# Query, key and value tensors laid out on the host, and sparse attention steps split in two, in a block-sparse attention and cosine-MLP kernel

## The chip, the cores and the metric

The kernel runs on one core of one Trainium2 chip. The metric is the time that the device needs for one execution, in microseconds (us), taken as the median of three runs. Lower is better. The host's own work ahead of the launch is not in it.

## The reference, cut to what matters

Attention over 4 batches, 8 heads, 768 tokens and 64 features a head, in float32. Tokens come in 24 blocks of 32. Each block of queries sees its own and its two neighbour blocks, the first and the last block, and three sampled blocks; the first and the last block of queries see everything. Behind it stands a two-layer MLP with the activation h*cos(h).

```python
scores = (q @ k.T) / sqrt(64)            # q, k, v: [4, 8, 768, 64]
mask = |blk_i - blk_j| <= 1 or blk_i in (0, 23) or blk_j in (0, 23) or blk_j in sampled_blocks[blk_i]
attn = softmax(where(mask, scores, -1e9)); x = attn @ v      # -> [3072, 512]
h = x @ w_in;  out = (h * cos(h)) @ w_out                    # w_in [512, 2048], w_out [2048, 512]
```

## The kernel before, in words

**Precision.** Every operand of a matmul is scaled by a power of two and split into two float16 parts, high and low; a product is the sum of high*high, high*low and low*high. So each stationary operand is loaded and streamed three times. The scale is found from the sum of squares (or a Gram matrix) of the tile.

**Tiles.** There are 24 query tiles of 128 rows, n = 0 to 23, six a batch: five sparse ones and a dense one (the first block and the last three). Two query tiles make one MLP step m = 0 to 11. A sparse tile has four units of two heads, a dense one eight units. A unit goes through scores (`qk`), adding the bias and taking the row maximum (`mx`, VectorE), exponential (`ex`, ScalarE), split into high and low (`ph`, `pl`), transpose (`PT`, by DMA; for the first sixteen units by TensorE, `PF`), and values (`pv`). The MLP of a step is 16 products up (`m`), the activation (`ev`, `ka`, `kb`, `sin`, `gm`, `gh`, `gl`) and 16 products down (`d`).

**Scores and values in two parts.** A sparse unit's scores are `shared_scores`, which read the neighbour and end blocks straight from the key tile `W` in tiles of 64 rows by 128 columns of the array, and `own_scores`, which read the sampled blocks from a gathered copy `Wg` in tiles of 64 by 32. Values have the same two parts, `shared_values` (128 by 128) and `own_values` (96 by 32), the latter reading V rows that GpSimd gathers by indirect DMA. Before, both parts are one step, `sparse_scores` or `sparse_values`, and `Plan.run` swaps the two inside a step where the part that comes first then has the tile shape of the work ahead of it.

**Layouts before.** q, k and v lie in HBM as the reference has them, [batch, head, token, feature], so that a row on a partition is put together from runs of 64 floats (256 bytes). The score matmul wants features on partitions. Keys of batch 0 are turned by TensorE (`KF0_0` to `KF0_5`, four float32 transposes each, L1832 through `turn32`); keys of batches 1 to 3 are scaled and split as they are into `kn` (`khi`, `klo`, 12 of each a batch) and turned by DMA (`kT`, L1353). Queries of tiles 0 to 3 are turned by TensorE (`UF`), those of tiles 4 to 23 by DMA (`uT`, L1449). A query's scale stands for one row.

**Order.** Engines take their instructions in program order. All loads, stores and DMA transposes are issued from SyncE's queue, gathers from GpSimd's. The order of all 3,183 steps is written out in the table `PLACES`, a name and its place, which `Plan.run` sorts by; buffers are dealt out in that order from the slots of `Sizes`. The numbers beside an `op` call are a planner's costs and due times; a step that has a place there is not moved by them.

Of the kernel before, what the change touches and what calls it, by code (L numbers as in the profile page):

```python
# [21 lines left out]
P = 128  # L22
BLK = 32
# [37 lines left out]
wl0 0 wc0_0 1 wc0_1 2 idx 3 const_ident 4 const_w 5 wc0_2 6 sx 7 regs2_0 8 kload0_1 9 KF0_2 10 const_samples 11 regs0_1 12 ql0 13 kload0_0 14  # L61
kload0_0#2 15 qsq0 16 kload0_1#2 17 const_pool 18 UF0 19 wsq0 20 KF0_1 21 const_a 22 kload0_2 23 kload0_2#2 24 ksq0_0 25 qsc0c 26 qsc0e 27 qsc0s 28
ql1 29 const_gidx 30 qhi0 31 ksq0_1 32 ksq0_2 33 qlo0 34 regs0_0 35 kred0 36 kall0s 37 regs3_1 38 kall0 39 ksc0c 40 ksc0e 41 vload0_0 42 regs4_1 43
qsq1 44 ksc0s 45 khi0_None_2 46 KF0_3 47 const_b1 48 vload0_2 49 KF0_4 50 qsc1c 51 KF0_5 52 khi0_None_3 53 qsc1e 54 KF0_0 55 vload0_1 56 khi0_None_1
57 qu0 58 klo0_None_2 59 khi0_None_4 60 klo0_None_3 61 khi0_None_5 62 klo0_None_1 63 vsq0_0 64 wl2 65 vsq0_1 66 khi0_None_0 67 klo0_None_4 68
klo0_None_5 69 klo0_None_0 70 vsq0_2 71 UF1 72 vred0 73 wl3 74 regs1_1 75 wgd0 76 wga0 77 vall0s 78 vall0 79 qnu0 80 ql2 81 vsc0c 82 qk0_0 83 vsc0e 84
vsc0s 85 vhi0_2 86 vlo0_2 87 wl4 88 const_b 89 wc3_0 90 mx0_0_0 91 vhi0_3 92 qk0_2 93 qk0_1 94 mx0_0_1 95 vst0_2 96 nb0_0 97 vhi0_4 98 vlo0_4 99
vhi0_5 100 vhi0_1 101 qsc1s 102 vlo0_5 103 qsq2 104 vhi0_0 105 vlo0_3 106 ex0_0_0 107 ex0_0_1 108 wl1 109 mx0_2_0 110 mx0_2_1 111 UF2 112 PF0_0_0 113
ql3 114 vst0_4 115 vlo0_1 116 PF0_0_1 117 nb0_2 118 const_n 119 ph0_0_0 120 vst0_5 121 vlo0_0 122 wc3_1 123 ex0_2_0 124 vst0_0 125 regs2_1 126 mx0_1_0
127 mx0_1_1 128 nb0_1 129 wc3_2 130 PG0_0_0 131 qk0_3 132 mx0_3_0 133 ph0_0_1 134 wc1_0 135 vst0_3 136 wc1_1 137 PG0_0_1 138 regs1_0 139 ex0_2_1 140  # L70
pg0_0_0 141 UF3 142 ex0_1_1 143 wc1_2 144 mx0_3_1 145 qsq3 146 qsc2c 147 qsc2e 148 ex0_1_0 149 qsc3c 150 vst0_1 151 wl6 152 const_c 153 wl7 154
PF0_2_0 155 pg0_0_1 156 PF0_1_0 157 ph0_2_0 158 PG0_2_0 159 qsc2s 160 wgd1 161 regs4_0 162 PF0_1_1 163 wsq1 164 wsq3 165 qsc3e 166 qhi1 167 nb0_3 168
wc7_0 169 wga1 170 qlo1 171 regs3_0 172 wc7_1 173 ex0_3_0 174 PF0_2_1 175 ex0_3_1 176 wred0 177 wall0s 178 wall0 179 wsc0c 180 qu1 181 ph0_1_0 182
PG0_1_0 183 ph0_1_1 184 ph0_2_1 185 PG0_1_1 186 qhi2 187 qsc3s 188 wsc0e 189 wsc0s 190 qnu1 191 ql4 192 qsq4 193 qsc4c 194 pg0_2_0 195 vg0_0 196
turn0_0 197 PG0_2_1 198 qsc4e 199 qsc4s 200 qk1_0 201 wc7_2 202 wl5 203 pg0_1_1 204 qu4 205 pg0_2_1 206 qk1_1 207 mx1_0_0 208 mx1_0_1 209 wc5_0 210
vg0_1 211 qlo2 212 qk1_3 213 nb1_0 214 whi2 215 mx1_1_0 216 mx1_1_1 217 qk1_2 218 qhi4 219 vi0_2 220 nb1_1 221 wsq7 222 whi0 223 vi0_0 224 wc5_1 225
wgd2 226 ex1_0_0 227 PF0_3_0 228 ex1_0_1 229 PF0_3_1 230 pg0_1_0 231 vi0_3 232 vg0_2 233 wsi0 234 vi0_1 235 qhi3 236 ex1_1_0 237 pv0_0 238 mx1_3_0 239
pv0_1 240 pv0_2 241 mx1_3_1 242 wc5_2 243 ph0_3_0 244 ph0_3_1 245 PG0_3_0 246 rs0 247 wl25 248 PG0_3_1 249 mx1_2_0 250 mx1_2_1 251 vg1_0 252 wlm0 253
wlm1 254 rr0 255 wga2 256 pg0_3_1 257 PF1_0_0 258 PF1_0_1 259 qu2 260 pg0_3_0 261 qlo4 262 qk2_0 263 wlp0 264 nb1_2 265 wsq5 266 qlo3 267 qnu4 268
pv0_3 269 vi1_0 270 ph1_0_0 271 ex1_1_1 272 ex1_2_1 273 wred4 274 wall4s 275 wl8 276 vi1_2 277 PF1_1_0 278 PG1_0_0 279 vi1_1 280 ph1_0_1 281 wall4 282  # L80
# [1933 lines left out]
```

## Time and profile before

| | |
|---|---|
| runs, median of 3 | 773.91 us (773.72 to 774.16) |
| profiled execution, its own time | 771.64 us |
| its span in the trace | 769.7 us |
| mean granted TensorE clock | 0.971 of full speed |
| busy: TensorE matmul, VectorE, ScalarE | 722.5, 618.8, 639.0 us |

The profiled execution lies 0.3% under the median; its span is what the trace covers. Busy shares are means over stages with different limits, and matmuls are pipelined, so a busy TensorE is not one at its peak. A row of a window gives the busy time of each engine in a stretch, the number of instructions, the granted clock, and the busy share of the 16 DMA engines.

### The profile page before, as it was taken

The page shows a single profiled execution, that of the slowest core. Times are in us where ns is not written, and L with a number is a line of the kernel's source. Part 1 is how long each engine was busy: PE and PEld are TensorE (multiplying, and loading weights), DVE is VectorE, ACT ScalarE, POOL GpSimd, SP SyncE. Part 2 cuts the span into 40 slices and gives each one's busy share as a digit, 9 for nine tenths or more (in the row PEclk, how much of TensorE's full clock was granted, in tenths as well). Part 3 has the DMA queues.
Part 4 walks back from the last instruction along what each step waited for, and adds up shares of the span by engine and source line. Part 5 has one row for each costly group of instructions (what it writes and reads, how often), then busy time and mean ns, then how long its engine had stood idle before and what let it go on. Part 6 is the DMA issues. An engine that isn't in the chain of part 4 may idle for free.

```text
span 769.7 us, 25139 instructions
## 1 busy us (share of the span) xinstructions
PE 722.5 (94%) x10330; PEld 497.3 (65%) x10330; DVE 618.8 (80%) x1578; ACT 639.0 (83%) x1260; POOL 98.2 (13%) x132
## 2 busy tenths in 40 slices
PE   5679998999999969999999999999999999999997
PEld 4456674667476537767576676667577776665673
DVE  4977999999979986989888798977878777776252
ACT  3789999999769987999799999989889887875152
POOL 4232102002300212010201202020202020000000
PEclk9659999999999999999999999999999999999999
DMA  9788995799959999999999999998899949366111
GB/s 215 257 228 233 251 264 114 165 235 220 189 115 183 184 156 203 222 262 160 192 213 177 223 206 233 208 185 153 158 163 184 179 95 166 100 129 105 28 42 42
DMA packets 289139, 135.41 MB, mean 176 GB/s; under 512 B 247680, under 2 KB 269312, under 8 KB 289024
## 3 DMA queue, kind: packets, MB, share of 16 engines
q1 hardware_dynamic: 283904, 118.07, 78.3%
q0 software_dynamic: 5120, 15.73, 8.4%
q8 instruction: 81, 1.33, 0.7%
q14 instruction: 34, 0.28, 0.1%
HBM read 68.23 MB, written 12.58 MB: 105 GB/s over the span
## 4 chain that ended last, share of the span: by engine, by line
PE 44%; ACT 24%; DVE 17%; DMA 9%; issue 5%; SPq 2%; DVEq 0%; ACTq 0%
PE ph L1885 18%; PE ph L1935 17%; ACT P L1586 6%; DMA xT<-n 3%; DVE P L1565 3%; ACT hs L1894 3%; ACT ring L1596 2%; DVE ring L1600 2%; PE ph L1663 2%; DMA PT<-ring 2%; ACT Wg L1359 2%; ACT g L1912 2%; DMA w<-in_moe_w_out_dram 2%; DVE hs L1917 1%; DMA U<-n 1%
## 5 line engine op out<-in xcount | busy, mean ns | idle before, releaser
L1885 PE MATMUL ph<-xT,w 128*128 128x256 f16 x2304 | 269.9, 275 | 10.1 <-DMA xT<-n 8.5
L1935 PE MATMUL ph<-w,g 128*128 128x512 f16 x1152 | 265.6, 380 | 0.2 <-DVE g L1926 0.2
L1885 PEld LDWEIGHTS <-w 128*128 128x128 f16 x2304 | 224.0, 99 | 50.7 <-issue 12.8
L1935 PEld LDWEIGHTS <-g 128*128 128x128 f16 x1152 | 108.8, 98 | 120.9 <-issue 4.8
L1586 ACT ACTIVATE P<-P,sm 128x352 f32<-128x352 f32 (+1 forms) x224 | 154.9, 698 | 4.8 <-DVE sm L1580 3.9
L1474 POOL DMA_INDIRECT V<-scr,gidx x80 | 86.4, 1080 | 523.9 <-PE ph L1647 369.5
L1600 DVE TENSOR_TENSOR ring<-P,ring 128x704 f16<-128x704 f32 (+1 forms) x96 | 86.6, 907 | 17.3 <-ACT ring L1596 16.0
L1894 ACT ACTIVATE hs<-ph,sm 128x512 f32<-128x512 f32 x96 | 62.8, 681 | 30.7 <-PE ph L1885 27.0
L1565 DVE CUSTOM_DVE_ANT_1 P<-ph,bias 128x352 f32<-128x352 f32 x160 | 79.3, 516 | 4.3 <-PE ph L1534 2.0
L1596 ACT CAST ring<-P 128x704 f16<-128x704 f32 (+1 forms) x96 | 75.1, 791 | 1.8 <-DMA PT<-ring 1.2
L1917 DVE SCALAR_TENSOR_TENSOR hs<-hs,sm,g 128x1024 f32<-128x1024 f32 x48 | 61.4, 1279 | 18.4 <-ACT g L1912 17.8
L1926 DVE TENSOR_TENSOR g<-hs,g 128x1024 f16<-128x1024 f32 x48 | 58.2, 1219 | 18.4 <-ACT g L1923 18.4
L1912 ACT ACTIVATE g<-g,sm 128x1024 f32<-128x1024 f32 x48 | 54.8, 1146 | 20.0 <-DVE g L1908 19.6
L1923 ACT ACTIVATE g<-hs 128x1024 f16<-128x1024 f32 x48 | 49.9, 1048 | 13.4 <-DVE hs L1917 13.4
L1908 DVE SCALAR_TENSOR_TENSOR g<-g,hs 128x1024 f32<-128x1024 f32 x48 | 58.4, 1220 | 0.6
L1904 DVE TENSOR_SCALAR g<-hs 128x1024 f32<-128x1024 f32 x48 | 33.1, 689 | 29.5 <-ACT hs L1894 26.8
L1586 ACT ACTIVATION_READ_ACCUMULATOR P<-P,sm 128x1 f32 x224 | 46.4, 207 | 0.0
L1526 PE MATMUL ph<-W,U 64*128 64x192 f16 (+1 forms) x960 | 42.5, 222 | 1.9 <-DVE sm L1565 1.9
L1663 PE MATMUL ph<-V,PT 128*128 128x64 f16 x960 | 42.4, 195 | 1.2 <-DMA PT<-ring 1.1
L1663 PEld LDWEIGHTS <-PT 128*128 128x128 f16 x960 | 36.4, 99 | 9.9 <-DMA PT<-ring 1.6
L1526 PEld LDWEIGHTS <-U 64*128 64x128 f16 x960 | 28.7, 96 | 17.1 <-issue 14.3
L1565 DVE CUSTOM_DVE_ANT_1 P<-ph,dbias 128x384 f32<-128x384 f32 x64 | 34.1, 551 | 4.3 <-PE ph L1549 3.8
(170 smaller groups left out, 870.2 us busy)
## 6 DMA issues: line engine op xcount, KB each, us to landing
V<-scr SPq DMA_DIRECT2D x20, 384.0 KB, 5.3
w<-in_moe_w_in_dram SPq DMA_DIRECT2D x12, 512.0 KB, 4.8
w<-in_moe_w_out_dram SPq DMA_DIRECT2D x12, 512.0 KB, 5.0
V<-scr SPq DMA_DIRECT2D x8, 768.0 KB, 4.8
scr<-n SPq DMA_DIRECT2D x21, 256.0 KB, 4.4
qs<-in_q_dram SPq DMA_DIRECT2D x20, 256.0 KB, 5.1
stage<-in_v_dram SPq DMA_DIRECT2D x9, 512.0 KB, 5.6
stage<-in_k_dram SPq DMA_DIRECT2D x9, 512.0 KB, 6.2
```

The source lines that it names most:

```text
L1474: self.nc.gpsimd.indirect_dma_start(V[:96, 2 + j, :], None, self.scr[b][:, :], bass.IndirectOffsetOnAxis(ap=self.gidx[:96, c : c + 1], axi ...
L1526: mm(out, u[r], x, start=(begins and first and not part), stop=(not begins and final and part == 1), tile_position=(a * D, 0))
L1565: self.nc.vector.tensor_tensor_reduce(out=self.p_view(n, Pt)[:, a].rearrange("p (n c) -> p n c", c=hf), in0=self.flat32(sp)[:, :w].rearran ...
L1586: self.nc.scalar.activation(Pv[:, a], Pv[:, a], AF.Exp, scale=qc[:, 4:5], bias=nb[:, a : a + 1], accum_out=sums[:, x : x + 1],)
L1596: self.nc.scalar.copy(R[:, :, 0, : self.width(n)], self.p_view(n, Pt))
L1600: self.nc.vector.tensor_tensor(R[:, :, 1, :w], self.p_view(n, Pt), R[:, :, 0, :w], ALU.subtract)
L1663: mm(xp[:, h, :], PT[:, 6 * a + 3 * l + c, :], V[:, c, h, d0:d1], start=(first and a == 0 and c == 0 and x == 0), stop=(not first and a == ...
L1885: self.nc.tensor.matmul(ph[:, ff, :], self.W1[p][:, wl, cc, c * P : (c + 1) * P], xT[:, xl * NCC + cc, :], start=(j == 0), stop=(j == len( ...
L1894: self.nc.scalar.activation(hs[:, h * 512 : h * 512 + 512], ph.rearrange("p f t -> p (f t)"), AF.Copy, scale=self.turns[b][:, p : p + 1])
L1912: self.nc.scalar.activation(kt, kt, AF.Sin, scale=-SIN_SCALE, bias=self.halfpi)
L1917: self.nc.vector.scalar_tensor_tensor(hs, hs, c[:, p : p + 1], kt, op0=ALU.mult, op1=ALU.mult)
L1935: self.nc.tensor.matmul(self.flat32(po), g[:, gl, ff, t * P : (t + 1) * P], self.W2[p][:, wl, ff, :], start=(first and ff == half * hf and ...
```

## The change

The host lays the three tensors out before the launch: q as [batch, tile, 128 partitions, 512], where a partition holds one of two heads' 64 features; k as [batch, 3, 128, 1024] with features on partitions; v as [batch, 3, 128, 1024] with tokens on partitions. A load is then one run of 2 or 4 KB a partition. All turning of q and k goes: 6 `KF`, 4 `UF`, 20 `uT`, 36 `kT`. A query tile is split straight into `U`, and keys into `W`, in 6 steps a batch for `khi` and `klo` each (12 before, for batches 1 to 3). Since a partition no longer is a query row, a query tile has one scale: its sums of squares are added over the partitions by a matmul with ones (`qsp`, 24 new steps on TensorE), whose result `row_scale` reads from PSUM. `qk` and `pv` of sparse units are two steps each (`qk`, `qo` and `pv`, `po`), placed apart; the first and the last of a PSUM bank get the start and stop flags. Slots: `qs` 1 to 2, `kn` 2 to 0, `ot` 2 and `acc` 2 to `ot` 5. `PLACES` is a new table of 3,258 steps.

```diff
-wl0 0 wc0_0 1 wc0_1 2 idx 3 const_ident 4 const_w 5 wc0_2 6 sx 7 regs2_0 8 kload0_1 9 KF0_2 10 const_samples 11 regs0_1 12 ql0 13 kload0_0 14
...
+ql1 0 idx 1 ql0 2 qsq1 3 sx 4 const_pool 5 kload0_0 6 qsq0 7 qsp0 8 qsp1 9 kload0_1 10 const_samples 11 qsc0c 12 qsc1c 13 kload0_2 14 ksq0_0 15
...
-            if not b:
-                for t in range(HT):
-                    op("SP", 0, pos + 0.01 * c, lambda st=st, c=c, t=t: e.k_load_turned(st.t, c, t), w=[(st, c * HT + t)], dma=1.0, name=f"kload{b}_{c}")
-            else:
-                op("SP", 0, pos + 0.01 * c, lambda st=st, c=c: e.kv_load(b, 0, st.t, c), w=[st], dma=1.73, name=f"kload{b}_{c}")
+            op("SP", 0, pos + 0.01 * c, lambda st=st, c=c: e.kv_load(b, 0, st.t, c), w=[st], dma=1.27, name=f"kload{b}_{c}")
...
+        for c, st in enumerate(kst[b]):
+            p_ = pos + 0.2 * c
+            op("ACT", 0.613, p_, lambda st=st, c=c: e.k_hi(b, half, c, st.t), r=[st, sk[b]], w=[(W, (half, c))], name=f"khi{b}_{half}_{c}")
+            op("DVE", 0.663, p_, lambda st=st, c=c: e.k_lo(b, half, c, st.t), r=[st, sk[b], (W, (half, c))], w=[(W, (half, c))], name=f"klo{b}_{half}_{c}")
...
+        qs, U, qc, sp = Val("qs"), Val("U"), Val("qc"), Val("ph")
+        op("SP", 0, pos, lambda: e.q_load(n, qs.t), w=[qs], dma=0.635, name=f"ql{n}")
+        op("ACT", 0.613, pos, lambda: e.q_square(qc.t, qs.t), r=[qs], w=[am], name=f"qsq{n}")
+        op("PE", 0.07, pos, lambda: e.q_sum(qc.t, sp.t), r=[am, sx], w=[sp], name=f"qsp{n}")
+        row_scale(pos, lambda x: e.q_scale(x, qc.t, sp.t), sp, (qc, "e"), qe, f"qsc{n}")
...
-            op("SP", 0, pos, lambda: e.u_transpose(U.t, qn.t), r=[qn], w=[U], dma=1.15, name=f"uT{n}")
...
-                op("PE", 0.692, pos, lambda own_first=False, j=j, sp=sp: e.sparse_scores(n, j, U.t, T["Wg"].t, [x.t for x in sp], own_first),
...
+                op("PE", 0.343, pos, lambda begins, ends, j=j, sp=sp: e.shared_scores(n, j, U.t, [x.t for x in sp], begins, ends),
...
+                op("PE", 0.158, pos + 0.01, lambda begins, ends, j=j, sp=sp: e.own_scores(j, U.t, T["Wg"].t, [x.t for x in sp], begins, ends),
...
+    def q_sum(self, c, sp):
+        one = self.one.bitcast(BF16)[:, 1:2].to_broadcast([P, P])
+        self.nc.tensor.matmul(self.flat32(sp)[:, 0:1], one, c[:, 0:1].bitcast(BF16)[:, 1:2], start=True, stop=True)
...
+def lay_out(name, a):
...
+    if name == "q":
+        a = np.roll(a, -BLK, axis=2).reshape(B, H // 2, 2, S // P, P, D)
+        a = a.transpose(0, 3, 2, 5, 1, 4).reshape(B, S // P, P, H // 2 * P)
+    elif name == "k":
+        a = a.reshape(B, H // 2, 2, S // 2, 2, D).transpose(0, 1, 2, 5, 4, 3).reshape(B, H // 2, P, S // 256, 256)
+        a = a.transpose(0, 3, 2, 1, 4).reshape(B, S // 256, P, H // 2 * 256)
```

## Rows read from the trace of the kernel before

**Rows 1.** The page: busy time of each engine, share of the span, instructions.
```profile
PE 722.5 (94%) x10330; PEld 497.3 (65%) x10330; DVE 618.8 (80%) x1578; ACT 639.0 (83%) x1260; POOL 98.2 (13%) x132
```

**Rows 2.** Windows: length; PE, PEld, DVE, ACT, POOL busy; granted clock; DMA share; GB/s.
```profile
0.00:60.00 60.00, 39.38 (x545) 29.16 (x545) 43.35 (x155) 39.94 (x95) 20.31 (x60) 0.74 0.92 235
60.00:200.00 140.00, 131.35 (x1928) 90.94 (x1927) 132.43 (x323) 136.04 (x279) 17.15 (x16) 0.99 0.85 206
200.00:220.00 20.00, 16.67 (x92) 9.54 (x91) 16.61 (x37) 12.49 (x26) 5.78 (x5) 0.91 0.92 208
...
280.00:300.00 20.00, 14.70 (x318) 11.13 (x294) 12.86 (x43) 12.50 (x29) 0.00 (x0) 0.83 1.02 167
300.00:770.00 470.00, 461.71 (x6421) 318.65 (x6417) 357.98 (x845) 383.28 (x714) 47.55 (x45) 1.00 0.86 160
```

**Rows 3.** Timeline of the first 25 us: start, us, engine, line, operation, tiles.
```profile
0.72 0.41 SPq L1755 DMA_DIRECT2D w<-in_moe_w_in_dram  x1
...
2.75 7.38 SPq L1329 DMA_DIRECT2D stage<-in_k_dram  x5
5.51 0.43 DVE L1763 TENSOR_SCALAR w<-w 128x512 int32<-128x512 int32 x1 [5.51 <-DMA w<-in_moe_w_in_dram]
...
14.24 0.61 PE L1255 MATMUL ph<-stage 128*128 128x128 bf16 x4 [0.37 <-DMA stage<-in_k_dram]
...
17.19 4.79 DVE L1244 SCALAR_TENSOR_TENSOR W<-ph,sm,W 128x256 f16<-128x256 f32 x12 [0.40 <-ACT W L1241]
...
22.43 0.51 PE L1526 MATMUL ph<-W,U 64*128 64x192 f16 x12
```

**Rows 4.** DMA issues on the page: KB each, median us from issue to landing.
```profile
w<-in_moe_w_in_dram SPq DMA_DIRECT2D x12, 512.0 KB, 4.8
...
stage<-in_k_dram SPq DMA_DIRECT2D x9, 512.0 KB, 6.2
```

**Rows 5.** Groups by shape: busy us, mean ns of one, idle before and releasers.
```profile
L1241 ACT ACTIVATE kn<-stage,sm 128x256 f16<-128x256 f32 x36 | 16.7, 498 | 3.2 <-DMA out_dram<-kn 2.5 <-DMA W<-kn 0.7
...
L1244 DVE SCALAR_TENSOR_TENSOR kn<-stage,sm,kn 128x256 f16<-128x256 f32 x36 | 16.4, 479 | 1.9 <-ACT kn L1241 1.9
...
L1244 DVE SCALAR_TENSOR_TENSOR n<-stage,sm,n 128x512 f16<-128x512 f32 x18 | 13.2, 748 | 2.0 <-ACT n L1241 1.9
L1227 ACT ACTIVATE n<-qs 128x512 bf16<-128x512 f32 x20 | 12.8, 640 | 1.4 <-DMA qs<-in_q_dram 1.4
L1241 ACT ACTIVATE n<-stage,sm 128x512 f16<-128x512 f32 x18 | 12.7, 711 | 1.9 <-DMA xT<-n 1.9
...
L1832 PE MATMUL ph<-acc,stage 128*128 128x128 f32 x24 | 5.8, 424 | 8.0 <-DMA stage<-in_k_dram 8.0
...
L1272 PE MATMUL ph<-ident,sm 128*128 128x128 f16 x16 | 3.7, 231 | 5.3 <-DVE sm L1258 4.2 <-DVE sm L1265 0.7 <-DVE sm L1786 0.3
```

**Rows 6.** Timeline: the two long idle times of TensorE behind 200 us.
```profile
213.33 1.05 PE L1885 MATMUL ph<-xT,w 128*128 128x256 f16 x7 [2.95 <-DMA xT<-n]
...
288.13 3.14 PE L1885 MATMUL ph<-xT,w 128*128 128x256 f16 x14 [5.30 <-DMA xT<-n]
```

**Rows 7.** The xT tile: time of its DMA transposes from issue to landing.
```profile
DMA to landing us min/median/max: 3.2/5.3/9.9
```

**Rows 8.** The U tile: issue of its DMA transposes on SyncE, ns least, median, most.
```profile
L1449 SPq DMA_TRANSPOSE U<-n x20: 1231/1405/5736, 92.3 to 628.3; - x20
```

**Rows 9.** The same for the W tile.
```profile
L1353 SPq DMA_TRANSPOSE W<-kn x36: 1190/1217/2291, 214.8 to 539.6; - x36
```

**Rows 10.** Timeline of TensorE in a stretch without waits.
```profile
506.77 0.51 PE L1663 MATMUL ph<-V,PT 128*128 128x64 f16 x12
507.21 0.56 PE L1647 MATMUL ph<-V,PT 96*32 96x64 f16 x48
...
517.05 0.69 PE L1679 MATMUL ph<-V,PT 128*128 128x64 f16 x18
517.58 1.46 PE L1935 MATMUL ph<-w,g 128*128 128x512 f16 x6
```

More of the change, by code (lines that the diff above doesn't have):

```diff
@@ L65 @@
[L65 to L68, printed above, removed]
@@ L398, in run @@
         self.order = sorted(self.ops, key=lambda o: (o.turn, o.n))
-        now = 0
+        banks = collections.defaultdict(list)
         for o in self.order:
-            if o.eng == "PE":
-                if o.swap and now == o.mode[1]:
-                    o.fn, o.mode = functools.partial(o.fn, True), o.mode[::-1]
-                now = o.mode[1]
+            if o.bank is not None:
+                banks[o.bank].append(o)
+        for ops in banks.values():
+            for o in ops:
+                o.fn = functools.partial(o.fn, o is ops[0], o is ops[-1])
         place = {id(o): k for k, o in enumerate(self.order)}
@@ L659, in gather_k @@
         for h0, h1 in halves:
-            part = [(W, (h, t)) for h in range(2) if h0 <= h * HH < h1 for t in range(NT)]
+            part = [(W, (h, t)) for h in range(2) if h0 <= h * HH < h1 for t in range(NT // HT)]
             f = 1.0 if h1 - h0 == H else 0.0
@@ L684, in attend, with values @@
         x = 0.034 if not sparse else 0.0
+        def values(j, vpos, PT):
+            bank = ("xp", n)
+            op("PE", 0.36, vpos, lambda begins, ends: e.shared_values(2 * j, PT.t, V.t, e.heads(xp.t), begins, ends),
+               r=[PT] + [(V, k) for k in range(len(e.v_parts(i)))], w=[(xp, (j, "s"))], name=f"pv{n}_{j}", bank=bank)
+            op("PE", 0.197, vpos + 0.01, lambda begins, ends: e.own_values(2 * j, PT.t, V.t, e.heads(xp.t), begins, ends),
+               r=[PT] + [(V, 10 + k) for k in range(4)], w=[(xp, (j, "o"))], name=f"po{n}_{j}", mode=(1, 1), bank=bank)
         def after_max(j, pos, vpos, Pt, R, PT, nb):
@@ L701, in after_max @@
                     raise ValueError
-                op("PE", 0.652, vpos, lambda last=False: e.sparse_values(2 * j, PT.t, V.t, e.heads(xp.t), last),
-                   r=[PT, V], w=[(xp, 2 * j), (xp, 2 * j + 1)], name=f"pv{n}_{j}", mode=(1, 0), swap=True)
+                values(j, vpos, PT)
                 return
@@ L917, in feed_forward @@
         pos_ = [None] * TT
-        acc = [Val("acc" if m else "kn") for _ in range(TT)] if early else None
+        acc = [Val("ot") for _ in range(TT)] if early else None
         for p in range(NWI):
@@ L1525, in shared_scores, with own_scores @@
                         out, x = spv[:, :, 0:96], keys[r, :, 64 * i : 64 * i + 96]
-                    mm(out, u[r], x, start=(begins and first and not part), stop=(not begins and final and part == 1), tile_position=(a * D, 0))
-    def own_scores(self, unit, U, Wg, sp, begins):
+                    mm(out, u[r], x, start=(begins and first and not part), stop=(closes and final and part == 1), tile_position=(a * D, 0))
+    def own_scores(self, unit, U, Wg, sp, begins, ends):
+        sp = [self.flat32(x) for x in sp]
         D, mm = self.D, self.nc.tensor.matmul
@@ L1538, in own_scores @@
                         start=(begins and first),
-                        stop=(not begins and final),
+                        stop=(ends and final),
                         tile_position=(a * D, 32 * j),
@@ L1666, in shared_values @@
                         V[:, c, h, d0:d1],
-                        start=(first and a == 0 and c == 0 and x == 0),
-                        stop=(not first and a == 1 and c == 1 and x == len(terms) - 1),
+                        start=(begins and a == 0 and c == 0 and x == 0),
+                        stop=(ends and a == 1 and c == 1 and x == len(terms) - 1),
                     )
```

791 lines of the change are left out of this document (321 added, 470 removed).

## The prediction

> **What bounds the kernel now.** I read the page first: TensorE is busy for 94% of the span, ScalarE for 83%, VectorE for 80% [rows 1]. These are averages, so I cut the span into windows [rows 2], and it falls into three stages. In the first 60 us no engine is full: TensorE 39.4, VectorE 43.4, ScalarE 39.9 of 60, and the granted clock is 0.74, so that TensorE stands at its lower level, 1.2 GHz, for about half of the stretch. From 60 to 200 us ScalarE (136.0 of 140) and VectorE (132.4) are both full: they convert weights, and TensorE takes what they give. From 300 us on TensorE is full, 461.7 of 470, at full clock; of the 8.3 us left some 4 are the tail. Between 200 and 300 us lie two holes, 200 to 220 and 280 to 300, where all three engines go idle together.
>
> So the end is set by TensorE, which has a fixed amount of products to do, and time can be won only where it stood idle or slow earlier, or where work is taken from it. What it lost before 300 us is about 39 us of idle time (60 - 39.4, 140 - 131.4, 3.3, 1.3 and 5.3) and, at half clock for half of the first 60 us, the work of perhaps 10 us more. That is the purse the change can draw on.
>
> **The head.** The first scores start at 22.43 us [rows 3]. The chain to them: five of the six key loads keep SyncE's queue for 7.38 us, to 10.13; the last keys have landed by 14.24, where their Gram matrix starts; the scale follows, and VectorE's twelve low parts fill W from 17.19 to 21.98.
>
> After the change the queue holds two query loads, the index load and three key loads ahead of the values. The nearest row for the issue of a load with long runs is the weights', 0.41 us [rows 3], so the third key load is issued by 0.7 + 6 x 0.41 = 3.2 us and the queue no longer sets the pace; the transfer does. It has 2 x 256 KB + 3 x 512 KB = 2.1 MB to bring. One weight load of 0.52 MB took from 0.72 to 5.51. At the 235 GB/s of the first 60 us 0.52 MB are 2.2 us, so 2.6 us of those 4.8 are fixed lag. The keys are then there at 0.7 + 2.6 + 2.1/0.235 = 12.2 us. That is the slow end, since those 235 GB/s were moved mostly in runs of 256 bytes. With long runs a 512 KB load lands in 4.8 against 6.2 us at the median [rows 4]; 0.77 of 8.9 us gives 10.2. I take 11: 3 us earlier than 14.2, bounds 2 and 4.
>
> The page "DMA: Bandwidth & Descriptors" of the Trainium skill (Specifications) says that transfers under 512 bytes miss line rate, and gives 358 GB/s as the limit of HBM for a core. By that figure, as an estimate, the keys would land at about 9.2 us, and the sum below would be 2 us larger. No run here shows that rate.
>
> Behind the landing, the first scores now need half of W only: three high parts and three low parts of 128x512, 0.71 + 3 x 0.75 = 3.0 us by the nearest rows [rows 5], where W took 5.5 (16.46 to 21.98, the high part's start being 0.71 before the first low). The gathers want both halves, 0.71 + 6 x 0.75 = 5.2, so there only 0.3 is won. The values' loads, queued behind the keys, also come about 5 us sooner, and the weights behind them. First scores 5.5 us earlier, gathers 3.3: I take 6 for the head, including the earlier weights, bounds 1 and 9. I let it through to the end, since the full ScalarE and VectorE of 60 to 200 us [rows 2] then start their queue of work earlier. Most of the rest is hidden: the 24 turns of keys on TensorE cost 5.8 us busy [rows 5] and the 16 turns of queries are like them, but TensorE waits in the head anyway. I count 1 us of it for the turns that came later than the first scores (0 to 3).
>
> **The holes behind 200 us.** In both, TensorE waits for the xT transpose of the first MLP step of the next pair: 2.95 and 5.30 us [rows 6]. One of these DMAs took 9.9 us against a median of 5.3 [rows 7], and the 16 DMA engines were over 90% busy in both windows [rows 2], the queue being full of transposes for U and W. The change takes 20 transposes of U and 36 of W from SyncE's queue, 20 x 1.41 + 36 x 1.22 = 72 us of issue [rows 8, 9], and their traffic. If the xT transposes come down to the median, 9.9 - 5.3 = 4.6 us of the second hole go, and of the first in proportion 1.4; the clock, which dipped to 0.83 and 0.91 there, comes back with them (half of 0.17 x 20 + 0.09 x 20, 2.6). That would be 8.6 at most. A shorter wait only uncovers the next late thing (the high and low parts of that tile), so I take 5.5, bounds 0 and 8.6.
>
> **Work in the middle.** Keys of batches 1 to 3: ScalarE 36 x 0.498 becomes 18 x 0.711, -5.1 us; VectorE 36 x 0.479 becomes 18 x 0.748, -3.8 us [rows 5]. From 300 us on this lies under TensorE and is worth nothing; if that cover were gone it would be worth those 5.1 and 3.8. Only batch 1's third, prepared around the holes, counts: 1 us (0 to 2).
>
> **Tile shapes.** Twelve products of L1663 take 0.44 us where the shape of the tile changes behind them (507.21 - 506.77), eighteen of the same kind in L1679 without such a change 0.53 (517.58 - 517.05), or 0.0294 each [rows 10]. 12 x 0.0294 = 0.35, so a change of shape costs 0.09 us. Counting them along the two tables, with the swap inside a step done as `Plan.run` does it, I get 299 before and 271 after, since `qo` and `po` of several units now stand side by side. 28 x 0.09 = 2.5 us off TensorE, nearly all in its full stretch. The number of products is the same.
>
> **What is added.** 24 `qsp` products stand in TensorE's queue between ScalarE's squares (0.64 us [rows 5]) and VectorE's three scale steps. The trace has no such step, but L1272 is its like, a small product between two other engines, 16 times: 0.231 us of latency each, and TensorE idle for 5.3 us before them, 0.33 each [rows 5]. Everything behind `qsp` waits with it: the up and down products of the MLP, hence `ev` on ScalarE. The bounds are 24 x 0.03 = 0.7 us (it streams one column, like the shortest products above) and 24 x 0.33 + 0.7 = 8.6. Most query tiles are prepared long before they are used, so the wait can have been placed where the squares are done; I take 24 x 0.1 = 2.4. The PSUM slot that it holds, the 2.5 us that ScalarE lost to the `kn` buffers [rows 5], and the second `qs` slot I cost at nothing: TensorE covers them.
>
> **Sum.** 6 + 1 + 5.5 + 1 + 2.5 - 2.4 = 13.6 us. The profiled execution took 771.6 with a span of 769.7; it would take 758.0. The median of the runs, 773.9, lies 2.3 higher, so I predict 760 us. What the new table does to all other waits can't be priced from rows; TensorE's idle time from 60 to 200 us is 8.7 and from 300 us on 8.3 [rows 2], and I allow 6 us either way.
>
> **Rivals.**
>
> The head's gain is swallowed. ScalarE and VectorE are full from 60 to 200 us, and if the first weights come no sooner (0.92 of the DMA engines' time is taken in the first 60 us), the earlier scores only make a longer pause before. Then 6 + 1 are lost: 767, or 770 if half of the holes stays too. For it: full engines after the head. Against it: in the head they are idle for 20.1 and 16.7 of 60 us, so there is room to pull work forward.
>
> TensorE comes up to 2.4 GHz sooner. At 0.74 for 60 us it lost up to 16 us of work; if denser work early brought back two thirds of that, 10 to 12 us, the time would be about 748. For it: all that feeds it comes sooner. Against it: the head's pace is set by other engines.
>
> The clock stays low for longer. With the turns gone, TensorE has longer pauses in the head. If the half clock then lasted for 10 us more, 5 us of work would be lost: 765, inside my forecast's own range. The page "TensorE: Matmul & The Clock Gate" of the Trainium skill (Why this matters for your kernels) says that idle gaps between bursts bring the clock back to half; the dips to 0.91 and 0.83 in the two holes agree.
>
> Slower: `qsp` stalls TensorE. If each of the 24 waits for a full square and then as long as the like steps did, 0.64 + 0.33, TensorE loses 24 x 0.97 = 23 us, most of it in its full stretch, where I counted 2.4: 781. It decides from (773.9 - 760 + 2.4)/24 = 0.68 us a wait. For it: strict order, and ScalarE 82% busy from 300 us on [rows 2]. Against it: 0.33 in the like steps.
>
> **Chances and range.** My forecast with its own range, 752 to 766: 0.50. Clock low for longer, 762 to 768: 0.07. Head swallowed, 766 to 773: 0.18. Clock up sooner, 742 to 752: 0.15. `qsp` stalls, 773 to 785: 0.10. The range 746 to 772 leaves out the slower case and the ends of its neighbours, under 0.2 in all. A measurement of this kernel can tell 0.2%, 1.5 us, from no change: faster 0.86 (0.50 + 0.07 + 0.15 and 0.14 of the swallowed case), same 0.05 (0.04 of that one and 0.01 of the slow case), slower 0.09.
>
> **What would show it.** First scores (L1526 there) at 16 to 18 us instead of 22.43; key loads with issues of about 0.4 us; TensorE's waits for xT behind 200 us under 2 us together; VectorE and ScalarE busy 4 to 6 us less; the wait before `qsp` under 0.1 us each. The prediction is wrong if the full stretch of ScalarE and VectorE ends no earlier than 200 us, if TensorE's clock in the first 60 us is far from 0.74, or if new waits of TensorE stand behind 300 us.

## The result and the profile after

The changed kernel takes 747.24 us (745.0 to 749.54, four runs) against 773.82 us for the kernel before on the same chip: a ratio of 0.967, 95% interval 0.962 to 0.972, or 26.6 us less. The forecast was 760 us, with a range of 746 to 772. So the sign is right and the time lies near the low end of the range; the gain is near twice the 13.9 us that I counted. The profiled execution took 748.22 us with a span of 746.2, 23.5 us less than the span before. A ratio, here and below, leaves out runs in which a kernel was in a second, slower state, so it need not be the quotient of the two medians beside it.

The page's line of busy times, which answers to [rows 1]:

```profile
PE 705.2 (95%) x10314; PEld 485.3 (65%) x10314; DVE 609.5 (82%) x1555; ACT 644.6 (86%) x1248; POOL 115.7 (16%) x132
```

The windows of the changed kernel, columns as in [rows 2]:

```profile
0.00:60.00 60.00, 34.57 (x634) 24.23 (x635) 44.34 (x164) 45.03 (x108) 32.20 (x63) 0.97 0.86 265
60.00:200.00 140.00, 130.68 (x1821) 88.43 (x1820) 133.54 (x313) 137.19 (x275) 23.48 (x16) 1.00 0.74 196
200.00:220.00 20.00, 19.67 (x217) 14.82 (x215) 19.86 (x62) 16.51 (x38) 3.13 (x3) 1.00 0.65 164
220.00:280.00 60.00, 59.70 (x1148) 37.98 (x1148) 55.73 (x172) 58.69 (x124) 7.59 (x8) 1.00 0.84 158
280.00:300.00 20.00, 20.00 (x412) 17.36 (x409) 19.38 (x52) 19.61 (x39) 4.35 (x4) 1.00 1.05 229
300.00:746.00 446.00, 440.59 (x6101) 302.45 (x6099) 336.64 (x797) 367.55 (x670) 44.93 (x40) 1.00 0.74 145
```

What to see: ScalarE and VectorE are still full from 60 to 200 us (137.2 and 133.5 of 140). From 200 us on TensorE is full at once: in the 100 us that held the two holes it is idle for 0.63 us (0.33 + 0.30 + 0.00) where it was idle for 9.97 (3.33, 1.34, 5.30), and the clock, which stood at 0.91 and 0.83 in the two short windows, is 1.00. That is 9.3 us of idle time. What the clock cost besides can be read from the kernel before's two stretches at half clock, the second cut in two where TensorE starts again (columns as above):

```profile
213.99:217.40 3.41, 3.41 (x19) 2.41 (x17) 2.46 (x7) 1.56 (x4) 0.00 (x0) 0.50 1.04 267
285.67:288.13 2.46, 0.00 (x0) 0.03 (x1) 2.29 (x16) 0.60 (x3) 0.00 (x0) 0.50 1.27 87
288.13:292.50 4.37, 4.37 (x21) 3.05 (x22) 2.44 (x7) 2.49 (x7) 0.00 (x0) 0.50 1.09 244
```

TensorE worked for 3.41 + 4.37 = 7.8 us at half clock and lost half of that, 3.9 us; the 2.46 us between are idle time already counted. So 13.2 of the 23.5 us were won in these 100 us.

The head, in the timeline (start, us, engine, line, what, idle time before it), as in [rows 3]:

```profile
2.11 1.38 SPq L1218 DMA_DIRECT2D stage<-in_k_dram  x3
...
10.23 1.03 PE L1191 MATMUL ph<-stage 128*128 128x128 bf16 x8 [0.24 <-DMA stage<-in_k_dram]
...
16.57 1.04 PE L1369 MATMUL ph<-W,U 64*128 64x192 f16 x16
21.27 0.61 PE L1369 MATMUL ph<-W,U 64*128 64x192 f16 x8 [3.66 <-DVE W L1180]
...
23.38 0.82 PE L1369 MATMUL ph<-W,U 64*128 64x192 f16 x12
...
51.62 0.51 PE L1369 MATMUL ph<-W,U 64*128 64x192 f16 x12
```

Three key loads take 1.38 us of SyncE's queue, the last keys are there at 10.23 us (14.24 before), and the first scores start at 16.57 (22.43 before). The next scores then wait 3.66 us for the low part of the second half of the keys.

How far this head is carried can be read from one step that both kernels have: the low part of the output of query tile 5, on VectorE, behind which the first hole opened. Before, and after:

```profile
204.97 0.67 DVE L1706 TENSOR_TENSOR n<-ot,n 128x512 f16<-128x512 f32 x1
```

```profile
199.76 0.68 DVE L1535 TENSOR_TENSOR n<-ot,n 128x512 f16<-128x512 f32 x1
```

It comes 5.2 us earlier. So by stage: 5.2 us up to 200 us, some 13.2 from there to 300, and the remaining 5.1 behind that, where TensorE is idle for 2.4 us less (469.7 - 461.7 = 8.0 before, 446.2 - 440.6 = 5.6 after).

### The profile page after: what moved, and what is told of

Same layout as the page of the kernel before. It is cut to its first block, busy times and chain, and to the rows that moved or that the text cites. A ratio compares the mean times of both kernels' runs of the same rounds, so it can differ in the third digit from the quotient of the medians.

```text
span 746.2 us, 24904 instructions
## 1 busy us (share of the span) xinstructions
PE 705.2 (95%) x10314; PEld 485.3 (65%) x10314; DVE 609.5 (82%) x1555; ACT 644.6 (86%) x1248; POOL 115.7 (16%) x132
## 4 chain that ended last, share of the span: by engine, by line
PE 56%; ACT 16%; DVE 15%; DMA 6%; issue 4%; SPq 0%; DVEq 0%; ACTq 0%
PE ph L1764 23%; PE ph L1714 21%; ACT P L1430 4%; PE ph L1369 2%; DVE P L1409 2%; PE ph L1492 2%; DMA PT<-ring 2%; DVE ring L1444 2%; ACT ring L1440 2%; PE ph L1378 2%; ACT junk L1163 2%; PE ph L1475 2%; PE ph L1508 2%; DMA scr<-n 1%; DVE g L1755 1%
## 5 line engine op out<-in xcount | busy, mean ns | idle before, releaser
L1714 PEld LDWEIGHTS <-w 128*128 128x128 f16 x2304 | 221.2, 98 | 36.8 <-issue 1.2
L1324 POOL DMA_INDIRECT V<-scr,gidx x80 | 95.8, 1198 | 477.8 <-PE ph L1475 331.8
L1430 ACT ACTIVATE P<-P,sm 128x352 f32<-128x352 f32 (+1 forms) x224 | 153.8, 691 | 11.2 <-DVE sm L1424 9.9
L1430 ACT ACTIVATION_READ_ACCUMULATOR P<-P,sm 128x1 f32 x224 | 44.6, 199 | 0.0
L1369 PE MATMUL ph<-W,U 64*128 64x192 f16 (+1 forms) x960 | 38.8, 224 | 4.7 <-DVE W L1180 3.7
L1492 PE MATMUL ph<-V,PT 128*128 128x64 f16 x960 | 39.8, 193 | 0.0
L1369 PEld LDWEIGHTS <-U 64*128 64x128 f16 x960 | 28.9, 97 | 16.7 <-issue 14.5
```

The lines of the kernel that those rows point to most:

```text
L1324: self.nc.gpsimd.indirect_dma_start(V[:96, 2 + j, :], None, self.scr[b][:, :], bass.IndirectOffsetOnAxis(ap=self.gidx[:96, c : c + 1], axi ...
L1369: mm(out, u[r], x, start=(begins and first and not part), stop=(closes and final and part == 1), tile_position=(a * D, 0))
L1430: self.nc.scalar.activation(Pv[:, a], Pv[:, a], AF.Exp, scale=qc[:, 4:5], bias=nb[:, a : a + 1], accum_out=sums[:, x : x + 1],)
L1492: mm(xp[:, h, :], PT[:, 6 * a + 3 * l + c, :], V[:, c, h, d0:d1], start=(begins and a == 0 and c == 0 and x == 0), stop=(ends and a == 1 a ...
L1714: self.nc.tensor.matmul(ph[:, ff, :], self.W1[p][:, wl, cc, c * P : (c + 1) * P], xT[:, xl * NCC + cc, :], start=(j == 0), stop=(j == len( ...
```

## The experiments

Twelve runs in three groups, each group on one chip beside the kernel before. The chips were not alike: the kernel before was slower on those of the first and third group than on that of the second, and so was the changed kernel on that of the third. So a run is compared within its group. The kernel before has a trace from the first comparison alone; where a trace below is set beside it, the two come from different chips.

| run | us | before there | ratio (95% interval) |
|---|---|---|---|
| 1: `e4_no_transposes` | 773.58 | 783.91 | 0.987 (0.977 to 0.997) |
| 1: `e1_old_order` | 816.36 | 783.91 | 1.042 (1.032 to 1.052) |
| 1: `e3_short_head` | 774.81 | 783.91 | 0.992 (0.988 to 0.996) |
| 1: `e6_filler` | 773.79 | 783.91 | 0.986 (0.974 to 0.999) |
| 2: `after_again` | 748.57 | 773.61 | 0.969 (0.961 to 0.977) |
| 2: `e8_old_no_sum` | 789.84 | 773.61 | 1.022 (1.014 to 1.030) |
| 2: `e7_no_sum` | 746.41 | 773.61 | 0.965 (0.957 to 0.972) |
| 2: `e2_together` | 753.85 | 773.61 | 0.974 (0.967 to 0.982) |
| 3: `e4b_no_transposes` | 774.20 | 785.44 | 0.987 (0.982 to 0.993) |
| 3: `e3b_short_head` | 776.41 | 785.44 | 0.988 (0.984 to 0.992) |
| 3: `e6b_filler` | 770.75 | 785.44 | 0.980 (0.972 to 0.988) |
| 3: `after_third` | 768.81 | 785.44 | 0.978 (0.974 to 0.982) |

**The changed kernel itself, twice more.** No edit.

> The changed kernel once more, beside the kernel before and the other runs of this call, so that differences of a few microseconds can be read on one chip. If the first comparison carries over, the ratio is 0.962 to 0.972. If the waits for TensorE's own queue that stood in the runs with a short-run head and with fillers (9 to 11 us behind 200 us, none in the first profile of the changed kernel) come from the chip and not from those edits, they stand here too, and the ratio is nearer to 0.98.

> The changed kernel again, so that the other three can be compared with it on one chip: a ratio of 0.962 to 0.977 to the kernel before, as in the two calls so far.

The second group repeats the first comparison (0.969). The third does not quite: there the changed kernel loses 20.2 us of its own (768.81 against 748.57), the kernel before 11.8. Most of what it loses them to stands in the last section.

**The transposes alone.** The kernel before, in its own order, without the issue of `uT` and `kT`:

```diff
-lambda t=t, kn=kn: e.k_transpose(b, half, t, kn.t)
+lambda: None
...
-lambda: e.u_transpose(U.t, qn.t)
+lambda: None
```

> The kernel before, with its order untouched, but the 56 transposing DMAs that bring U (20) and W (36) into place are not issued. Their targets keep the values of earlier tiles, so the scores of the later query tiles and of batches 1 to 3 are not computed from their own data; every other instruction is there. Theory A (the transposes on SyncE's queue made the two holes behind 200 us): TensorE's waits for xT between 200 and 300 us fall from 8.3 us to under 2, the granted clock shows no dip there, and the time falls by 12 to 17 us, to 757 to 762. Theory B (the new order closed the holes, and the transposes had little to do with it): the holes stay with at least 5 us of idle time, and the time is 768 or more. My forecast of 5.5 us for the holes would give 768.

> The kernel before without its 56 transposing DMAs into U and W, a second time, because in the first run TensorE also waited 3 us for its own queue behind 200 us and 3.6 us at 82.7 us, which the kernel before does not show in its profile. There the first hole stayed (2.60 us of 2.95), the second fell from 5.30 to 1.68 us and one of its two clock dips of 3.4 us was left. Theory A (the transposes are worth what closes in the second hole, my forecast's 5.5 us; the first hole and the rest of the gain belong to the order): 4 to 8 us faster than before, a ratio of 0.990 to 0.995. Theory B (the transposes carry most of the gain of the holes): 12 us or more, a ratio under 0.985.

Both runs give a ratio of 0.987, between the two theories. The waits of TensorE between 200 and 300 us in the second run (line, releaser: us in total, times, longest) and its windows:

```profile
PE ph L1885 <- DMA xT<-n: 3.5, 2, 2.2
```

```profile
200.00:220.00 20.00, 17.61 (x132) 9.13 (x130) 18.42 (x43) 14.69 (x28) 6.27 (x5) 0.95 0.79 185
220.00:280.00 60.00, 58.24 (x1007) 38.88 (x1004) 55.28 (x169) 53.33 (x116) 4.60 (x4) 0.99 0.70 124
280.00:300.00 20.00, 18.12 (x413) 13.16 (x417) 16.90 (x60) 17.00 (x41) 2.76 (x3) 1.00 1.15 206
```

The second hole is down from 5.30 to 1.88 us of idle time, with the clock whole; the first is as it was but for 1 us (2.39 for 3.33), with a dip still in it. In all 6.0 us of idle time stay of 9.97, and 1.7 of the 3.9 us of clock: without the transposes 6.1 us come back, a little under half of the 13.2. The other half is not theirs: nothing that SyncE's queue was rid of closes the first hole. The medians fall by more, 10.3 and 11.2 us; where the rest was won these traces do not show.

SyncE's queue in the kernel before shows why the first hole stays. TensorE sat idle from 210.38 to 213.33 and from 282.83 to 288.13 us:

```profile
196.91 1.44 SPq L1449 DMA_TRANSPOSE U<-n  x1
...
202.59 5.29 SPq L1725 DMA_TRANSPOSE xT<-n  x2
...
214.79 14.79 SPq L1353 DMA_TRANSPOSE W<-kn  x8
...
278.06 1.23 SPq L1725 DMA_TRANSPOSE xT<-n  x1
281.17 4.72 SPq L1633 DMA_TRANSPOSE PT<-ring  x1
```

Ahead of the first hole stand one transpose of U, over by 198.4 us, and none of W, whose first comes behind it. In the second hole none is being issued either, but xT is faster without them: issued at 278.06 us, it was there at 288.13, 10.1 us later; in the second run it was issued at 283.70 and there at 290.01, 6.3 us later. What in those 56 transposes held it back was not told apart.

**The order alone.** The changed kernel in the order of before, with and without the query's sum:

```diff
 def places():
-    (the new table)
+    (the table of the kernel before)
...
+        d[f"qsp{n}"] = d[f"qsc{n}c"] - 0.1
+            d[f"qo{n}_{j}"] = d[f"qk{n}_{j}"] + 0.1
+            d[f"po{n}_{j}"] = d[f"pv{n}_{j}"] + 0.1
...
+                    d[f"{x}{b}_{half}_{c}"] = max(d[f"{x}{b}_{h}_{2 * c + t}"] for t in range(2)) + 0.1 * half
```

The second run has besides

```diff
-        op("PE", 0.07, pos, lambda: e.q_sum(qc.t, sp.t), r=[am, sx], w=[sp], name=f"qsp{n}")
...
-        self.row_scale(x, self.flat32(sp)[:, 0:1], 2.0**-20, c[:, 1:2], c[:, 2:3], c[:, 3:4])
+        self.row_scale(x, c[:, 0:1], 2.0**-20, c[:, 1:2], c[:, 2:3], c[:, 3:4])
```

> The changed kernel with the order of the kernel before: every step stands at its old place, and the new ones follow from it (the query's sum just ahead of its scale, the own part of scores and of values right behind the shared part, each key step at the later of the two places it replaces). 16 of the new places then had to move back to where a buffer comes free. Theory A (layout and removed DMAs make the gain, the new order only trims): 750 to 757, with no hole of more than 2 us behind 200 us. Theory B (the new order makes it): 765 or more, and the holes stay. Between them, 757 to 765, both count. In either case the head is as early as in the changed kernel up to the first keys (their Gram matrix at 10 to 11 us instead of 14.24).

> The changed kernel in the order of before, as in the run with the old order (816 us), but without the 24 one-column products that sum the squares of a query tile over the partitions: each partition takes its own sum for the scale, so the scales are other numbers. In the run with the old order TensorE waited 19.7 us for the squares of six of them, and VectorE 33.3 us for the products. Theory A (in the old order it is this product that costs, the layout itself gains): the time falls under that of before, by 5 to 15 us, a ratio of 0.98 to 0.995. Theory B (the old order does not fit the new steps at all, whichever product is in it): still slower than before, a ratio over 1.01. For the holes: if they stay closed, the layout closed them; if TensorE waits over 4 us for xT between 200 and 300 us, the new order did.

Theory B has the direction in both, but neither theory of the first run foresaw this: in the old order the new steps are not a smaller gain but a loss of 4.2%, and of 2.2% without the sum. The sum is dear there; its line in the first of the two runs (duration, then what TensorE and others waited for, us and times):

```profile
L1304 PE MATMUL ph<-sm x24: 163/167/208, 11.0 to 663.6; 128*128 128x1 bf16 x24
its engine sat idle before it (us, times) until:
  ACT junk L1186: 19.7, 6
...
who waited for it (us, times):
  DVE sm L1191: 33.3, 14
```

By the two ratios it costs (1.042 - 1.022) x 774 = 16 us in that order. Their intervals leave 6 to 26 us, and the two runs stand in different groups, between which a kernel's ratio can differ (0.969 and 0.978 for the changed kernel), so this is an estimate. Without the sum, most of the loss is made ahead of tile 5: its step, shown above for the other two kernels, comes 10.3 us later than before, of 16.4 us by which the span is longer (786.1 against 769.7). That step, the windows, ScalarE's longest wait from 14 to 62 us, and the longest wait of SyncE's queue up to 62 us:

```profile
215.23 0.67 DVE L1557 TENSOR_TENSOR n<-ot,n 128x512 f16<-128x512 f32 x1
```

```profile
0.00:60.00 60.00, 25.25 (x397) 18.25 (x397) 37.47 (x130) 31.03 (x72) 25.22 (x60) 0.87 0.65 223
200.00:220.00 20.00, 19.66 (x170) 11.35 (x168) 18.94 (x40) 15.29 (x29) 5.20 (x5) 1.00 0.80 181
220.00:280.00 60.00, 55.21 (x938) 37.27 (x936) 53.45 (x155) 47.84 (x98) 4.31 (x4) 1.00 0.60 125
280.00:300.00 20.00, 17.02 (x349) 10.54 (x347) 17.23 (x65) 19.59 (x47) 2.76 (x3) 1.00 0.94 160
```

```profile
ACT junk L1185 <- DMA qs<-in_q_dram: 12.7, 2, 6.5
```

```profile
SPq L1296 <- DVE U L1202: 19.2, 3, 10.0
```

A raw query tile now keeps its `qs` slot until its low part is made, where a turned one let it go at the turn. In the old order the next query loads (L1296) wait for the low parts that free the slots, and ScalarE 12.7 us for the loads. And behind 200 us 8.1 us of idle time stay (0.34 + 4.79 + 2.98), though the transposes are gone and the clock holds. So their removal alone does not close the holes: the old order without the transposes keeps 6.0, the new steps in the old order 8.1 (other waits among them, since this kernel is 10 us behind there), and new steps and new order together leave 0.63. The new order with the transposes still in it was not run, and which of its moves closes the holes was not told apart. The loss behind tile 5 has a plain part: the two parts of a step stand side by side there without the swap, so the tile's shape changes 387 times, counted as in the prediction, 88 times more than before; at the 0.071 to 0.080 us estimated below that is 6 to 7 us.

**The head alone.** The first loads in runs of 256 bytes again, all else as changed:

```diff
+    def short_runs(self, dst, src, short):
+        if not short:
+            return dst, src
+        src = src.rearrange("p c -> (p c)").rearrange("(n p d) -> p n d", p=P, d=64)
+        return dst.rearrange("p (n d) -> p n d", d=64), src
...
-        self.nc.sync.dma_start(self.f32(st), (self.k, self.v)[w][b, c])
+        self.nc.sync.dma_start(*self.short_runs(self.f32(st), (self.k, self.v)[w][b, c], b == 0))
```

> The changed kernel, but the loads of batch 0's keys and values and of the first two query tiles are made of 256-byte runs again (the numbers land in other places, so batch 0 is computed from scrambled data; the amount of work is the same). The loads should take about 1.4 us of SyncE's queue each, the last keys' Gram matrix should start at 13 to 15 us instead of 10.23, and the first scores about 3.5 us later than 16.57. Theory A (the head's gain is swallowed by the full ScalarE and VectorE of 60 to 200 us): the end moves by less than 1.5 us, 747 to 749. Theory B (what the head wins reaches the end, as my forecast had it): the end moves by 3 to 5 us, 750 to 752.

> The changed kernel with 256-byte runs in the loads of batch 0's keys and values and of two query tiles, a second time, beside the changed kernel, since the first run stood on a chip on which the changed kernel was not run. (The numbers land in other places; the amount of work is the same.) Theory A (swallowed behind the head): under 1.5 us slower than the changed kernel in this call. Theory B (reaches the end): 3 to 5 us slower.

The first run has no changed kernel beside it. In the third group the end moves by 7.6 us (776.41 against 768.81; spans 773.8 and 768.8, so 5.0 between the two profiled executions). So the head is not swallowed; Theory B is right in kind, and by the medians too small. Its timeline:

```profile
2.31 5.93 SPq L1224 DMA_DIRECT2D stage<-in_k_dram  x3
...
13.48 1.03 PE L1191 MATMUL ph<-stage 128*128 128x128 bf16 x8 [1.35 <-DMA stage<-in_k_dram]
...
21.95 1.04 PE L1375 MATMUL ph<-W,U 64*128 64x192 f16 x16
```

A load takes 1.98 us of the queue instead of 0.46, and the first scores start at 21.95, where they stood before the change. So without the long runs nothing of the earlier scores is left. The keys account for 3.25 us of the 5.4 (13.48 against 10.23); the rest is the values' loads, whose Gram matrices stand ahead of the first scores in TensorE's order (the last of them starts at 20.31 us here, at 14.08 in the changed kernel). What moved, for the changed kernel from 4 to 12 us and for this one from 4 to 14 (packets of the DMA queues, bytes, rate, and how many packets are short):

```profile
DMA packets 943, 3.16 MB, mean 394 GB/s; under 512 B 101, under 2 KB 118, under 8 KB 943
```

```profile
DMA packets 8827, 2.25 MB, mean 225 GB/s; under 512 B 8793, under 2 KB 8827, under 8 KB 8827
```

**The clock in the head.** Products for nothing ahead of steps that wait (first 120 of them, also ahead of the queries' sums; then 50, elsewhere):

```diff
+        few = dict(qk0_2=24, PF0_0_0=12, PF0_1_0=14)
...
+        self.nc.tensor.matmul(self.flat32(t)[:, 0:P], self.ident, self.ident, start=True, stop=True)
```

> The changed kernel with work for nothing on TensorE in the head: ahead of each of ten steps between the keys' scale and the first turned probabilities stand twelve products of 128x128 that write a PSUM slot before it is used (120 products, about 13 us at 1.2 GHz). They only run where TensorE would wait. Theory A (TensorE's clock in the head does not set the end, since ScalarE and VectorE do): full clock comes some 10 to 18 us earlier than 37.8 us, and the time stays within 1.5 us of 747.2. Theory B (the low clock up to 37.8 us costs its lost work, some 19 us at half clock): the time falls by 4 to 9 us, to 738 to 743.

> The changed kernel with 50 products of 128x128 for nothing on TensorE, 24 ahead of the second pair of scores and 26 ahead of two turns of probabilities, where TensorE sat idle for 3.66, 1.37 and 1.84 us; they write a PSUM slot ahead of its use. In the earlier run with fillers, which also stood ahead of the queries' sums, full clock came at 15.1 us but did not last, and the attention fell 5 us behind. Theory A (the clock in the head does not set the end): full clock 5 to 12 us earlier, and the end within 1.5 us of the changed kernel in this call. Theory B (the low clock up to 37.8 us costs its lost work): 3 to 6 us faster.

The first run has no changed kernel beside it. The second ends 1.9 us later than the changed kernel of its group, within what its interval leaves open. Full clock stands from 19.4 to 22.8 and again from 33.1 us, against 36.6 us without the products, and up to 204 us TensorE and VectorE are 2.8 us ahead. It is lost in one place (TensorE's timeline):

```profile
203.83 0.17 PE L1294 MATMUL ph<-sm 128*128 128x1 bf16 x1
206.46 3.81 PE L1727 MATMUL ph<-xT,w 128*128 128x256 f16 x20 [2.47 <-DMA xT<-n]
```

The same product follows the same sum without a wait in the changed kernel of that group, at 206.79. TensorE came sooner to the first hole, and the hole was there again. The clock came up only for 3.4 us early, so this is a weak test of what a full clock in the head would give; it does show that such a lead need not pass 200 us.

**The query's sum, and the steps apart,** each in the new order. `e7_no_sum` has the second diff above; `e2_together`:

```diff
+            for x, y in (("qk", "qo"), ("pv", "po")):
+                d[f"{x}{n}_{j}"] = max(d[f"{y}{n}_{j}"], d[f"{x}{n}_{j}"])
+                d[f"{y}{n}_{j}"] = d[f"{x}{n}_{j}"] + 0.1
...
+            if pair and now == y.mode[0]:
+                self.order[a], self.order[b] = x, y = y, x
```

> The changed kernel in its own order without the same 24 products (each partition's own sum sets the scale, so the scales are other numbers). My forecast counted 2.4 us for them, the slower rival 23. By the changed kernel's trace (24 products of 0.167 us and about 13 us of idle time ahead of them, most of it in the head where TensorE waits anyway): 1 to 4 us faster than the changed kernel in this call. If the product stalled TensorE, 10 us or more.

> The changed kernel with the shared and the own part of every sparse score and value step side by side again, both at the later of their two places, and in the cheaper of the two sequences, as the kernel before did it. 136 of the 160 pairs stood apart. The shape of TensorE's tile then changes 337 times instead of 271: at 0.09 us a change that is 5.9 us more. Theory A (standing apart is worth its shape changes and little else): 5 to 8 us slower than the changed kernel in this call. Theory B (the split lets TensorE do the shared part while the gathered keys or values are still on their way, and that is where the unforecast gain is): 12 us slower or more, with new waits for Wg or for gathered V. Theory C (a change costs less than 0.09): under 3 us.

Without the sum 2.2 us less (746.41 against 748.57), with intervals that overlap and equal spans of 745.1: the sum costs between nothing and some 2 us here. In the changed kernel's trace 7.2 us of its wait stand ahead of the very first, where nothing else is to be done:

```profile
its engine sat idle before it (us, times) until:
  ACT junk L1163: 7.2, 1
...
  DVE sm L1409: 3.8, 2
```

Together again costs 5.3 us (spans: 749.8 against 745.1, 4.7). For 66 changes of shape more that is 0.071 to 0.080 us each, if it is all theirs. It is an estimate, since waits moved too: behind 300 us TensorE waits 2.2 us for `PT` in this run, once, and 1.1 us for `Wg` in the changed kernel, while the step of tile 5 comes 1.6 us earlier (197.78 against 199.39). Theory A: standing apart is worth about its shapes, and no new wait for `Wg` or `V` came.

## Why the prediction was right, and where its sizes were off

| term | forecast, us | measured, us |
|---|---|---|
| head, with earlier weights | 6 (1 to 9) | 5.2 at tile 5; 5.0 to 7.6 by the short runs |
| turns that came late | 1 (0 to 3) | not told apart; within the 5.2 |
| holes behind 200 us | 5.5 (0 to 8.6) | 13.2; the transposes alone 6.1 |
| middle work of ScalarE and VectorE | 1 (0 to 2) | not told apart |
| shapes of the tile | 2.5 | 28 x 0.071 to 0.080 = 2.0 to 2.2, an estimate |
| the query's sum | -2.4 (-0.7 to -8.6) | 0 to -2.2 |

**The term that was mis-sized is the holes:** 5.5 us in the sum, 13.2 measured. The transposes' own part came near the forecast: the second hole shrinks, and 6.1 us come back. But I misread how they act. I wrote that SyncE's queue was full of transposes for U and W in both windows; in neither hole was one being issued, and only the second answers to them. What I left out is the other part, some 7 us. I held that a shorter wait only uncovers the next late thing, and of the new table I said that it can't be priced, 6 us either way. With the new order all of the idle time went, in the first hole too, while the runs in the old order, from either kernel, keep 6.0 and 8.1 us of it. The lost clock was a small error: I halved 5.2 us to 2.6, and the stretches at half clock cost 3.9.

**The range.** The time, 747.24 us, lies below my forecast's own 752 to 766 and inside the 742 to 752 of "clock up sooner". The stated range reached down to 746 because of that rival, and its cause is not the one seen below; so that the range holds the time is in part luck.

**The head** came as forecast, keys at 10.23 (I had taken 11) and scores at 16.57 (16 to 18). The rate that I took, 235 GB/s, was that of short runs; long ones moved 394. Here the Trainium skill, "DMA: Bandwidth & Descriptors" (Specifications), holds where I weighed it against the trace: runs under 512 bytes miss line rate, 225 against 394 GB/s. Its 358 GB/s for a core were exceeded over those 8 us, so here they were no bound.

**The signs that I named.** Key loads of 0.46 us: right. TensorE's waits for xT behind 200 us: 0.2 us in all, against 8.3 in the two holes [rows 6]. VectorE is busy for 9.3 us less, but ScalarE for 5.6 us more [rows 1]: wrong as I put it. The new order makes ScalarE load its activation tables 51 times where the old one, with old or new steps, did so 45 times; at 1.28 us each that is 7.7 us, and without them it would be busy for 2.1 us less. The full stretch of ScalarE and VectorE still reaches 200 us, the sign that I had called fatal; it was not, since what it feeds at 200 us came 5.2 us sooner all the same. The clock of the first 60 us is no sign at all: 0.74 and 0.97 are both misread (last section). New waits behind 300 us did not come; the longest are 1.2 us for `Wg`, two together. Waits ahead of the sum: not 0.1 each, but the first of 7.2 us and two of 3.8 us together, the rest short.

**The rivals.** Head swallowed: refuted by the short runs, whose tile 5 is 5.6 us later than that of the changed kernel in the group (206.90 against 201.28, the same step as above) and whose span is 5.0 us longer. Clock up sooner: its time is the one that came, but most of the gain lies elsewhere, behind 200 us. In the first 60 us the changed kernel has some 9 us more of full clock (18.8 against 9.9 us, last section); that is at most 4.5 us of work, it is within the 5.2 of the head if it counts at all, and a lead of 2.8 us made with fillers was given back at 206 us. Clock low for longer: not seen, by the same figures. Sum stalls: not in this order, yet in the old one it cost 16 us by the two ratios (6 to 26), near the 23 of the rival. That where the step was put kept it small, as I had supposed, fits these two costs; no row shows it for a single step.

## What to carry to other kernels

A layout that removes work from a hand-ordered kernel is only half a change: with the old order this one was 2 to 4% slower, with its own 3% faster. In the old order queries' buffers were held longer, a new small product stood between engines, and the tile changed its shape more often. Where all engines go idle together, count the whole hole, and of the clock what was lost while TensorE worked; then ask separately what the transfer, the queue and the order each hold back, and look at what the queue issued just ahead of the hole. What is won in a head in which no engine is full can reach the end, even through a stretch where others are full, as long as what follows starts from it.

## What was not expected of the hardware

The same kernel took 748.57 us on one chip and 768.81 on another. In the slower run TensorE waits for nothing that the profile shows, in three places; between 220 and 620 us (waits, as above), and in the first place:

```profile
PE ph L1492 <- issue: 6.5, 14, 1.1
PE ph L1378 <- issue: 2.8, 6, 0.5
```

```profile
250.91 0.32 PE L1492 MATMUL ph<-V,PT 128*128 128x64 f16 x5 [0.48 <-issue]
251.67 0.32 PE L1492 MATMUL ph<-V,PT 128*128 128x64 f16 x3 [0.44 <-issue]
253.11 0.27 PE L1492 MATMUL ph<-V,PT 128*128 128x64 f16 x2 [1.13 <-issue]
```

A few products run, then a pause of about 0.4 us, over some 5 us, and the clock falls to half for 6.8 us. The waits of this kind between 220 and 620 us come to 11.4 us, and TensorE worked for 13.0 us at half clock in the three places, which cost half of that: about 18 of the 23.7 us by which the two spans differ (768.8 and 745.1). The runs with short loads and with fillers, on this chip and on that of the first group, show it near the same products. What holds the queue back was not tried.

In the changed kernel's window of 0 to 60 us the granted clock reads 0.97, but twelve products of L1369 take 0.82 us at 23.38 and 0.51 at 51.62 (timeline of the head, above): the first level on record there is that of 37.8 us, and what stands ahead of it is shown as full clock though it was the lower level. The 0.74 of the kernel before is too high for the same reason. Its record starts at 19.4 us, and ahead of that twenty products of L1255 take 2.34 us (at 11.54), where behind it eight take 0.63 (at 20.79). By the records, with the lower level ahead of them, the kernel before has full clock for 6.8 + 3.0 us of the 60 (from 19.4 and from 57.0) and the changed kernel for 10.3 + 8.5 (from 37.8 and from 51.5). The means of the two heads can't be compared; the durations can.
